# Holding the second group of first loads behind a mask product, and moving one transpose of the next batch behind the first output units, in a fused attention and feed-forward kernel

## The chip, the cores and the metric

The kernel runs on one core of a Trainium2 chip. A core has five engines with a queue of instructions each: TensorE (PE: matrix products and transposes, with its weight loads shown apart as PEld), VectorE (DVE), ScalarE (ACT), GpSimd (POOL) and SyncE (SP). They work at the same time and wait for each other by semaphores. Sixteen DMA engines move data between the large memory (HBM) and the on-chip memory (SBUF); products end in a small memory of their own (PSUM). The metric is the device time of one execution in microseconds (us); lower is better.

## What is computed

Eight batches of eight heads with 576 positions and 64 columns a head go through attention with a sliding window, and the result through a feed-forward layer without gate or bias:

```python
scores = scale * np.matmul(q, k.transpose(0, 1, 3, 2))
mask_plain = (rel >= 0) & (rel < 32)
mask_dil = (rel >= 0) & (rel < 128) & (rel % 4 == 0)
masks = [mask_plain if h < H // 2 else mask_dil for h in range(H)]
attn = softmax(where(masks, scores, -1e9))
x = (attn @ v) with the heads side by side      # 4608 tokens x 512
h = x @ w_in                                    # 512 -> 2048
out = (h * sigmoid(h)) @ w_out                  # 2048 -> 512
```

Half of the heads are "plain": a query sees the 32 positions up to its own. The other half is dilated: a query sees every fourth position, 32 of them. Positions with the same remainder modulo four form a class, and within a class a dilated head is a plain one of 144 positions.

## The kernel before

The order of all work is written out by hand (`tc.manual_schedule()`): each engine runs its instructions in the order in which the Python code issues them. In names of tiles and functions `z` is 0 for the plain heads and 1 for the dilated ones; `b` is the batch.

Attention is done in blocks of 32 queries against 64 keys. For each batch and each kind of head there are these steps: load q and k with a cast to 16 bits, turn them so that the 64 columns lie on partitions (`transpose`: TensorE transposes into PSUM, then a copy per half into `qT`, `kT` or `qC`, `kC`), products of queries and keys (`scores`), mask and row maximum on VectorE, exponentials on ScalarE (`exps`), normalisation and a transpose on VectorE (`normal`, `turned`), products with the values (`values`) and the copy of their result into `xT` (`finish`). The feed-forward layer of a batch has 16 hidden units (`layer1`, for batch 0 `layer1_part`, each 128 of the 2048 columns) with a Silu on ScalarE, and then output units (`layer2`, for batches 0 and 1 together four tiles of 128 tokens in `layer2_first`, 16 units of four products each).

A batch's attention is spread between the feed-forward products of the batch before it. `plan_of(b)` is a table of steps: `at(s, function, ...)` puts a piece of work ahead of unit `s`. Steps 0 to 15 stand ahead of the hidden units, 16 to 31 ahead of the output units; negative steps belong to batch 0 alone.

Batch 0 has nothing to hide behind, so its start is written out at the end of the kernel. Its q and k come in two parts of positions, 0 to 255 and 256 to 575 (`load_part`, into memory that later holds the hidden units, `gT`). The first products of a part add the mask: `mask0` multiplies a unit matrix with the tile `mask_b` into PSUM, and `scores0` adds the scores. The order of the first steps is: mask and scores of the dilated heads, then `mask0(0, 0)` and scores of the plain heads, transposes of k's second part, then of q's second part.

All loads are issued by GpSimd, in this order before the change: k and q of part 0, k of part 1, values of dilated heads 0 and 1, q of part 1, values of dilated heads 2 and 3 (`load_v1`), then values of plain heads 0 and 1 (`load_v0`), the first quarter of `w_in` (`load_w_in`), values of plain heads 2 and 3, two more quarters of `w_in`, and k of batch 1's dilated heads (`load_one`). Eight loads may be under way: a load waits for the landing of the one eight places before it. Everything later (`loads_held`) stands behind a tiny memset into a tile that VectorE and ScalarE use, so that GpSimd waits until that tile is no longer read:

```python
nc.gpsimd.memset(att(0)["l", 0, 1][0:1, 0:1], 0.0)
```

The lines that matter below: L135 `load_part`, L174 `load_v1`, L186 `load_v0`, L199 `load_w_in`, L298 the transposes of batches 1 and on, L302 their copies for plain heads, L335 the copies of batch 0, L392 plain scores, L426 masking, L453 `mask0`, L600 to L630 normalisation and transpose of probabilities, L661 value products, L704 filler products (`warm`), L765 and L786 hidden units of batch 0, L807 output units of batch 0, L859 the memset of `loads_held`.

Of the kernel before, what the change touches and what calls it, by code (L numbers as in the profile page):

```python
# [19 lines left out]
NEG = -1.0e9  # L20
# [9 lines left out]
def kernel(  # L30
# [9 lines left out]
    nc = tc.nc  # L40
    B, H, S, D = q.shape
    DM, DFF = moe_w_in.shape
    scale = 1.0 / (D ** 0.5)
# [32 lines left out]
    mask_b = cpool.tile([P, 2, KB], BF16, name="mask_b")  # L76
# [15 lines left out]
    def tiles_qk(b):  # L92

        for which in (0, 1):
            t = nat.tile([P, GN[0] * QB + GN[1] * GW], F16, tag=f"n{which}", name=f"n{which}_{b}")
            sq = [
                t[:, 0 : GN[0] * QB].rearrange("p (g e) -> p g e", e=QB),
                t[:, GN[0] * QB :].rearrange("p (g e) -> p g e", e=GW),
            ]
            t = t[:, 0 : 2 * sum(URS) * D].rearrange("p (u d) -> p u d", d=D)  # L100
            u0, u1 = 2 * URS[0], 2 * (URS[0] + URS[1])
            qk[b, 0, which] = t[:, 0:u0].rearrange("p (h u) d -> p h u d", h=2)
            qk[b, 1, which] = t[:, u0:u1].rearrange("p (h u) d -> p h u d", h=2)
            for z in (0, 1):
                if b >= DT[z]:
                    qk[b, z, which] = sq[z]

    def load_one(b, z, which):

        src = (q, k)[which]  # L110
        if z == 0:
            nc.gpsimd.dma_start(
                out=qk[b, z, which].rearrange("p h u d -> p h (u d)"),
                in_=src[b, z * HH : z * HH + HH].rearrange("(h i) (p u) d -> (i p) h (u d)", i=2, u=URS[z]),
            )
            return
        for i in (0, 1):
            h = HH + 2 * i
            nc.gpsimd.dma_start(
                out=qk[b, z, which][i * HF : i * HF + UPS[z]].rearrange("p h u d -> p h (u d)"),  # L120
                in_=src[b, h : h + 2].rearrange("h (p u) d -> p h (u d)", u=URS[z]),
            )
# [60 lines left out]
    def load_v0(b, heads=range(HH)):  # L183

        for h in heads:
            nc.gpsimd.dma_start(  # L186
                out=vws[b % 2][h * QB : h * QB + QB, 0:NB], in_=v[b, h].rearrange("(m p) d -> p m d", p=QB)
            )
# [9 lines left out]
    def load_w_in(c):  # L198
        nc.gpsimd.dma_start(  # L199
            out=w_in16[:, :, c * FC : (c + 1) * FC],  # L200
            in_=moe_w_in[:, c * FC : (c + 1) * FC].rearrange("(c p) f -> p c f", p=P),
        )
# [24 lines left out]
    load_v1(0, (0, 1))  # L227
    load_part(0, 1)
    load_v1(0, (2, 3))
    load_v0(0, (0, 1))  # L230
    load_w_in(0)
    load_v0(0, (2, 3))
    for c in (1, 2):
        load_w_in(c)
    tiles_qk(1)
    load_one(1, 1, 1)

    for kt, kc, qc in zip(kTs, kCs, qCs):
        nc.vector.memset(kc[:, :, :, 0:W], 0.0)
# [177 lines left out]
    def width(b, z, g):  # L417

        if b == 0:
            return 8 + g * (4 if z else 2)  # L420
        return 10 if z or g else 8
# [11 lines left out]
    def mask0(z, part, idle=0):  # L433

        n = (2, 3)[part]
        w = width(0, z, part)
        sd = big.tile([P, 16, KB], F32, tag="big", name=f"s0_{z}_{part}")
        bank = sd[:, 0:8].rearrange("p t c -> p (t c)")
        if z:
            sd = sd.rearrange("p (m t) c -> p m t c", m=2)  # L440
            if part:
                parts = [(sd[:, m, 0 : 2 * n], mask_b[:, 1:2].broadcast_to([P, 2 * n, KB])) for m in (0, 1)]
            else:
                pair = mask_b.rearrange("p t c -> p (t c)")[:, None, :].broadcast_to([P, 2, 2 * KB])
                parts = [(sd[:, m, 0:4].rearrange("p (e t) c -> p e (t c)", e=2), pair) for m in (0, 1)]
        elif part:
            parts = [(sd[:, o : o + x], mask_b[:, 1:2].broadcast_to([P, x, KB])) for o, x in ((0, 8), (8, 2))]
        else:
            parts = [(sd[:, 0], mask_b[:, 0]), (sd[:, 1:8], mask_b[:, 1:2].broadcast_to([P, 7, KB]))]
        for i, (t, x) in enumerate(parts):  # L450
            if i == 0:
                warm(bank, idle)
            nc.tensor.matmul(  # L453
                t, ident4.rearrange("p h q -> p (h q)"), x,
                start=bool(z or part or i == 0), stop=True, skip_group_check=not (z or part),
            )
        att(0)["s", z, part] = sd

    def scores0(z, part):

        n = (2, 3)[part]
        w = width(0, z, part)
        sd = att(0)["s", z, part]
        if z:
            for t in range(n):
                for e in (0, 1):
                    for h in range(HH):
                        for m in (0, 1):
                            score_class(0, h, 2 * e + m, 2 * part + t, sd[:, m, e * n + t], False)
        else:  # L470
            for j in range(w):
                for h in (0, 2, 1, 3):
                    score(0, h, 8 * part + j, sd[:, j], False)
        att(0)["raw", z, part] = sd[:, :, 0 : 2 * n] if z else sd[:, 0:w]
# [226 lines left out]
    def warm(t, n):  # L701

        for _ in range(n):
            nc.tensor.matmul(  # L704
                t, ident, ident[:, None, :].broadcast_to([P, 512 // P, P]),
                start=True, stop=True, skip_group_check=True,
            )
# [131 lines left out]
    dve, act = nc.vector.tensor_copy, nc.scalar.copy  # L839
    both = (dve, act)  # L840

    def transposes(at, b, z, step, copies=both):
        for which in (1, 0):
            if b >= DT[z]:
                at(step, turn_qk, b, z, which)
                continue
            at(step, transpose, b, z, which, copies)
# [20 lines left out]
    def plan_of(b):  # L868
        ev = {}

        def at(s, fn, *args):
            ev.setdefault(s, []).append((fn, args))

        def all_exps(b, z):
            for hi in (0, 1):
                at(16, exps, b, z, hi)

        if b == 0:

            at(-8, values0, 1, 1)  # L880
            at(-8, loads_held)
            at(-8, finish0, 1, 1, (act, dve))
            at(-6, values0, 0, 1)
            at(-6, finish0, 0, 1)
            at(0, build_mask)
            at(1, load_qk, 2)
            transposes(at, 1, 1, 6)
            at(10, scores, 1, 1, 0)
            at(11, scores, 1, 1, 1)
            at(13, transpose, 1, 0, 1, both)  # L890
            at(15, transpose, 1, 0, 0, both)
            at(11, shift, 1, 1, 0)
            at(17, scores, 1, 0, 0)
            at(19, scores, 1, 0, 1)
            at(15, load_qk, 3)
            at(15, load_v, 2)
            all_exps(1, 1)
            for hi in (0, 1):
                at(20, exps, 1, 0, hi)
            later(at, 1, 1, (20, 21, 24, 27), (act, act))  # L900
            later(at, 1, 0, (23, 24, 28, 31), (act, dve))
        elif b == 1:
            at(16, load_v, 3)
            transposes(at, 2, 0, 4)
            transposes(at, 2, 1, 6)
            at(10, scores, 2, 0)
            transposes(at, 3, 0, 11, (dve, dve))
            at(17, load_qk, 4)
            at(15, scores, 2, 1)
            all_exps(2, 0)  # L910
            all_exps(2, 1)
            at(17, scores, 3, 0)
            later(at, 2, 0, (21, 24, 27, 28))
            at(22, shift, 3, 0, 0)
            at(22, exps, 3, 0, 0)
            at(22, exps, 3, 0, 1)
            later(at, 2, 1, (29, 30, 33, 34), both)
        else:
            if b + 2 < B:
                at(16, load_v, b + 2)  # L920
            if b + 1 < B:
                later(at, b + 1, 0, (0, 0, 4, 6))
                transposes(at, b + 1, 1, 7)
                if b + 3 < B:
                    at(16, load_qk, b + 3)
            if b + 2 < B:
                transposes(at, b + 2, 0, 14)
                at(19, scores, b + 2, 0)
                at(20, exps, b + 2, 0, 0)
                at(20, exps, b + 2, 0, 1)  # L930
            if b + 1 < B:
                at(12, scores, b + 1, 1)
                if b + 2 == B:
                    at(14, shift, b + 1, 1, 0)
                all_exps(b + 1, 1)
                later(at, b + 1, 1, (22, 23, 27, 28))

        def plan(s):
            for fn, args in ev.pop(s, ()):
                fn(*args)  # L940

        return plan
# [15 lines left out]
    shift0(1, 0)  # L958
    exps(0, 1, 0)
    mask0(0, 0)  # L960
    scores0(0, 0)
    max0(0, 0)
    scaled(0, 0)
# [81 lines left out]
```

## Time and profile before

| | |
|---|---|
| time, median of 3 runs | 303.81 us (303.81 to 304.36) |
| the profiled execution's own time | 304.1 us |
| its span | 302.3 us |
| PE busy | 292.3 us, 97% |
| ACT busy | 203.3 us, 67% |
| DVE busy | 192.7 us, 64% |
| POOL busy | 118.9 us, 39% |
| first product of PE | 5.46 us |
| PE's share of the chain that ended last | 94% |

The span runs from the first to the last instruction; about 1.8 us of the execution lie around it. The first 5.5 us pass before the first load has landed. From then on PE is busy nearly without a break, so a time is gained or lost where PE waits in the first 55 us, and the later part only repeats. The page's forty slices tell nothing that fine; the chain in order of time and the timelines of the single engines do. A load's line shows GpSimd's time to issue it; its landing comes later, and is given as "us to landing". PE's own instructions are brought by a DMA queue too, queue 8 of the page.

### The profile page before, as it was taken

The page shows a single profiled execution, that of the slowest core. Times are in us where ns is not written, and L with a number is a line of the kernel's source. Part 1 is how long each engine was busy: PE and PEld are TensorE (multiplying, and loading weights), DVE is VectorE, ACT ScalarE, POOL GpSimd, SP SyncE. Part 2 cuts the span into 40 slices and gives each one's busy share as a digit, 9 for nine tenths or more (in the row PEclk, how much of TensorE's full clock was granted, in tenths as well). Part 3 has the DMA queues.
Part 4 walks back from the last instruction along what each step waited for, and adds up shares of the span by engine and source line. Part 5 has one row for each costly group of instructions (what it writes and reads, how often), then busy time and mean ns, then how long its engine had stood idle before and what let it go on. Part 6 is the DMA issues. An engine that isn't in the chain of part 4 may idle for free.

```text
span 302.3 us, 10281 instructions
## 1 busy us (share of the span) xinstructions
PE 292.3 (97%) x4395; PEld 186.0 (62%) x4395; DVE 192.7 (64%) x358; ACT 203.3 (67%) x684; POOL 118.9 (39%) x182
## 2 busy tenths in 40 slices
PE   2999999999999999999999999999999999999995
PEld 2667744677446774577545775477644775477543
DVE  1886669559997868776893768856893765800012
ACT  3677689775998659956894559975795568246200
POOL 8709228868898394427705095240000000000000
PEclk9999999999999999999999999999999999999999
DMA  8998999999999899499939199390002000210021
GB/s 103 172 200 124 192 202 137 219 150 138 134 162 184 96 84 147 96 100 51 132 81 160 37 69 132 108 119 2 2 35 106 37 2 23 84 37 0 13 94 69
DMA packets 113213, 30.47 MB, mean 101 GB/s; under 512 B 95520, under 2 KB 108688, under 8 KB 113168
## 3 DMA queue, kind: packets, MB, share of 16 engines
q0 software_dynamic: 107840, 20.38, 85.8%
q1 hardware_dynamic: 5328, 9.44, 8.7%
q8 instruction: 34, 0.56, 0.8%
q14 instruction: 11, 0.09, 0.1%
HBM read 40.75 MB, written 9.44 MB: 166 GB/s over the span
## 4 chain that ended last, share of the span: by engine, by line
PE 94%; DMA 2%; POOL 1%; issue 1%; ACT 0%; DVE 0%; POOLq 0%
PE o L831 37%; PE h L745 37%; PE h L786 5%; PE o L807 5%; PE x L661 4%; DMA gT<-in_q_dram 2%; PE s L382 2%; PE t L298 1%; PE s L392 1%; POOL gT L135 1%; PE h L765 1%; PE s L408 0%; PE ss L382 0%; POOL vw L174 0%; PE h L704 0%
## 5 line engine op out<-in xcount | busy, mean ns | idle before, releaser
L753 ACT ACTIVATE gT<-h 128x576 f16<-128x576 f32 x112 | 72.8, 650 | 63.2 <-PE h L745 63.1
L831 PE MATMUL o<-w_out,gT 128*128 128x512 f16 (+2 forms) x528 | 113.8, 373 | 0.0
L745 PE MATMUL h<-xT,w_in 128*128 128x288 f16 x896 | 113.2, 287 | 0.0
L745 PEld LDWEIGHTS <-w_in 128*128 128x128 f16 x896 | 86.4, 98 | 23.4
L831 PEld LDWEIGHTS <-gT 128*128 128x128 f16 x528 | 50.0, 98 | 56.1
L592 ACT ACTIVATE pe<-ms,nm 128x64 f32<-128x64 f32 x238 | 78.9, 333 | 0.1
L816 DVE COPY ob<-o 128x512 f32<-128x512 f32 (+2 forms) x35 | 23.0, 666 | 51.7 <-PE o L831 50.6
L592 ACT ACTIVATION_READ_ACCUMULATOR pe<-ms,nm 128x1 f32 x238 | 44.6, 187 | 0.0
L152 POOL DMA_DIRECT2D n<-in_k_dram x44 | 32.0, 744 | 26.4 <-DVE kC L355 24.0
L426 DVE SCALAR_TENSOR_TENSOR ms<-s,mask 128x512 f32<-128x512 f32 x28 | 19.2, 686 | 26.6 <-PE s L382 19.5
L152 POOL DMA_DIRECT2D n<-in_q_dram x44 | 32.1, 748 | 3.8 <-DMA n<-in_q_dram 2.2
L174 POOL DMA_DIRECT2D vw<-in_v_dram x32 | 18.3, 580 | 31.4 <-PE x L661 25.0
L614 DVE TENSOR_TENSOR pn<-pe,r 128x640 f16<-128x640 f32 (+2 forms) x32 | 25.3, 792 | 1.1
L630 DVE STREAM_TRANSPOSE pt<-pn 128x640 f16<-128x640 f16 (+4 forms) x32 | 24.7, 772 | 1.1
L186 POOL DMA_DIRECT2D vw<-in_v_dram x32 | 21.2, 674 | 9.0 <-DMA w_out<-in_moe_w_out_dram 8.9
L506 DVE TENSOR_REDUCE nm<-ms 128x10 f32<-128x640 f32 (+1 forms) x28 | 21.9, 786 | 0.9
L661 PEld LDWEIGHTS <-vw 32*64 32x64 f16 (+1 forms) x1264 | 12.9, 107 | 6.7 <-issue 5.4
L786 PE MATMUL h<-xT,w_in 128*128 128x320 f16 (+1 forms) x120 | 16.5, 288 | 0.0
L694 DVE CAST xT<-x 128x288 f16<-128x288 f32 x26 | 10.1, 450 | 8.2 <-PE x L661 8.2
L661 PE MATMUL x<-pt,vw 32*64 32x64 f16 (+2 forms) x1264 | 14.9, 193 | 0.4 <-issue 0.4
L807 PE MATMUL o<-w_out,gT 128*128 128x512 f16 x64 | 14.7, 380 | 0.0
L786 PEld LDWEIGHTS <-w_in 128*128 128x128 f16 x120 | 11.1, 98 | 3.3 <-DMA w_in<-in_moe_w_in_dram 0.2
(102 smaller groups left out, 207.5 us busy)
## 6 DMA issues: line engine op xcount, KB each, us to landing
out_dram<-ob SPq DMA_DIRECT2D x35, 256.0 KB, 3.4
n<-in_k_dram POOLq DMA_DIRECT2D x24, 108.0 KB, 5.0
n<-in_q_dram POOLq DMA_DIRECT2D x24, 108.0 KB, 4.8
vw<-in_v_dram POOLq DMA_DIRECT2D x31, 80.0 KB, 4.1
vw<-in_v_dram POOLq DMA_DIRECT2D x32, 72.0 KB, 4.2
w_in<-in_moe_w_in_dram POOLq DMA_DIRECT2D x4, 512.0 KB, 8.5
w_out<-in_moe_w_out_dram POOLq DMA_DIRECT2D x4, 512.0 KB, 14.9
n<-in_k_dram POOLq DMA_DIRECT2D x20, 72.0 KB, 5.1
```

Source lines behind the costliest of these rows:

```text
L152: nc.gpsimd.dma_start(out=qk[b, z, which][o : o + QB], in_=bass.AP((q, k)[which].tensor, (b * H + z * HH + half * HH // 2) * S * D + x * Q ...
L506: nc.vector.tensor_reduce(out=nm[:, 0:w], in_=ms[:, 0:w], axis=AX.X, op=ALU.max, negate=True)
L592: nc.scalar.activation(pe[:, t, :], src[t], AF.Exp, bias=a["nm", z, hi][:, t : t + 1], scale=k, accum_out=l[:, t : t + 1],)
L614: nc.vector.tensor_tensor(pn[:, 0:w], a["pe", z, hi][:, 0:w], r[:, 0:w, None].broadcast_to([P, w, KB]), ALU.mult)
L630: nc.vector.transpose(out, src)
L661: nc.tensor.matmul(x[h // 2][h % 2 * D : h % 2 * D + D, col : col + wd], vws[b % 2][r, NB + kb * DIL + c if z else kb], turned_cols(b, pt[ ...
L745: nc.tensor.matmul(h[:, half, 0:HS], w_in16[:, c, f * P : f * P + P], xT[c // 2][:, c % 2, half * HS : half * HS + HS], start=(c == cs[0]) ...
L753: nc.scalar.activation(gT[:, f, s0 : s0 + S].rearrange("p (a c) -> p a c", a=2), h[:, :, 0:HS], AF.Silu)
L786: nc.tensor.matmul(hs[i // m][:, i % m, 0 : c1 - c0], w_in16[:, c, (f + i) * P : (f + i + 1) * P], xT[c // 2][:, c % 2, c0:c1], start=(c = ...
L807: nc.tensor.matmul(o, gT[:, f, t * P : (t + 1) * P], w_out16[:, f, :], start=(f == 0), stop=(f == NFF - 1),)
L816: copy(ob, o)
L831: nc.tensor.matmul(o[:, 0, 0:m], gT[:, f, t * P : (t + 1) * P], w_out16[:, f, cols], start=(f == 0), stop=(f == NFF - 1),)
```

## The change

Two edits. First, the loads from the plain values of batch 0 on are put into a function `loads_second`, which is called right after `mask0(0, 0)`. It begins with a memset by GpSimd of one element of `mask_b`, with the value that is there already. That element is read by the mask product, so GpSimd waits for the product before it issues those loads. The order of the loads among each other stays. Second, in batch 0's plan the transpose of batch 1's plain q goes from step 15 (ahead of the last hidden unit) to step 17 (ahead of the second output unit), and both of its copies are made by VectorE (`(dve, dve)`), where one was ScalarE's. The two halves of the plain scores go from steps 17 and 19 to 19 and 20.

```diff
     load_v1(0, (2, 3))
-    load_v0(0, (0, 1))
-    load_w_in(0)
-    load_v0(0, (2, 3))
-    for c in (1, 2):
-        load_w_in(c)
-    tiles_qk(1)
-    load_one(1, 1, 1)
+
+    def loads_second():
+
+        nc.gpsimd.memset(mask_b[0:1, 0, 0:1], NEG / scale)
+        load_v0(0, (0, 1))
+        load_w_in(0)
+        load_v0(0, (2, 3))
+        for c in (1, 2):
+            load_w_in(c)
+        tiles_qk(1)
+        load_one(1, 1, 1)
...
             at(13, transpose, 1, 0, 1, both)
-            at(15, transpose, 1, 0, 0, both)
+            at(17, transpose, 1, 0, 0, (dve, dve))
             at(11, shift, 1, 1, 0)
-            at(17, scores, 1, 0, 0)
-            at(19, scores, 1, 0, 1)
+            at(19, scores, 1, 0, 0)
+            at(20, scores, 1, 0, 1)
...
     mask0(0, 0)
+    loads_second()
     scores0(0, 0)
```

## The prediction

> **What bounds the kernel now.** I read the page first (busy shares, chain), then the chain in order of time, then the first 55 us engine by engine, because the chain holds no wait worth naming behind them.
>
> ```profile
> span 302.3 us, 10281 instructions
> PE 292.3 (97%) x4395; PEld 186.0 (62%) x4395; DVE 192.7 (64%) x358; ACT 203.3 (67%) x684; POOL 118.9 (39%) x182
> PE 94%; DMA 2%; POOL 1%; issue 1%; ACT 0%; DVE 0%; POOLq 0%
> q8 instruction: 34, 0.56, 0.8%
> ```
>
> TensorE (PE) carries 94% of the chain. Whatever the change does must show as PE work starting earlier or later; the last line is the queue that brings PE's own instructions, used below. The chain in order of time has three pieces that are not PE work once the first product has begun:
>
> ```profile
> 5.63 7.20 DMA gT<-in_q_dram
> ...
> 13.62 0.70 ACT qC L335
> ...
> 15.21 0.35 issue
> ...
> 39.07 0.44 issue
> ```
>
> The first is the load of q's second part, which lands at 12.82 and ends a PE gap of 0.54 us. The second and third are gaps in which PE waits for nothing that the page names. The trace's packets of queue 8 name it: each is 16 KB of PE's instructions, 256 of them. One ran from 13.20 to 14.17 and the gap ended at 15.57; another ran from 37.12 to 38.07 and the gap ended at 39.51. Both gaps end 1.4 us after a fetch does, and they fall on the instructions numbered 450 and 1474 of PE's stream, which lie 4 x 256 apart. So PE had run out of instructions. A fetch is asked for when PE crosses the boundary before (9.30 and 33.13 here) and started 3.9 and 4.0 us later, while the load queue was full; at 22.8, where it was nearly drained, the lag was nil. After 39.51 the chain is PE alone but for 0.02 us, so any shift that survives at 55 us is the change in the total.
>
> What POOL issues, and the one weight load of PE that waits for it:
>
> ```profile
> 7.50 1.34 POOL L186 DMA_DIRECT2D vw<-in_v_dram  x2
> 8.82 0.79 POOL L199 DMA_DIRECT2D w_in<-in_moe_w_in_dram  x1
> 9.57 1.35 POOL L186 DMA_DIRECT2D vw<-in_v_dram  x2
> 13.11 1.52 POOL L199 DMA_DIRECT2D w_in<-in_moe_w_in_dram  x2 [2.18 <-DMA gT<-in_q_dram]
> ```
>
> ```profile
> 21.52 1.64 PEld L786 LDWEIGHTS <-w_in 128*128 128x128 f16 x16 [0.20 <-DMA w_in<-in_moe_w_in_dram]
> ```
>
> The three w_in chunks land at 17.44, 21.48 and 23.64 (issue plus 8.6, 8.4 and 9.8 us to landing). PE wants them at 17.48, 21.44 and 24.00. The second one binds already: its first product starts at 21.53, 0.09 us late, and it is the point that decides how much of an early gain lives.
>
> VectorE (DVE) and PE around the moved transposes:
>
> ```profile
> 39.91 0.76 DVE L302 COPY qT<-t 128x576 f16<-128x576 f16 x1 [1.05 <-PE t L298]
> 41.80 0.69 DVE L426 SCALAR_TENSOR_TENSOR ms<-s,mask 128x512 f32<-128x512 f32 x1 [1.14 <-PE s L392]
> 43.98 0.69 DVE L426 SCALAR_TENSOR_TENSOR ms<-s,mask 128x512 f32<-128x512 f32 x1 [0.76 <-PE ss L392]
> 45.64 0.81 DVE L600 TENSOR_REDUCE l<-pe 128x10 f32<-128x640 f32 x1
> 49.84 0.85 DVE L630 STREAM_TRANSPOSE pt<-pn 128x640 f16<-128x640 f16 x1
> ```
>
> ```profile
> 50.91 0.88 PE L661 MATMUL x<-pt,vw 32*64 32x64 f16 x80
> ```
>
> From 45.64 on DVE runs without a pause to the transposed probabilities at 50.69. PE's value products start 0.22 us after that; their first 20 use the half that was ready at 48.63, the rest the one of 50.69. This slack is small.
>
> **Part one, the loads held.** Added: one GpSimd memset (0.09 us, the 1x1 memset of line 859) and its wait for PE's plain mask product, which ends at 9.21 (8.61 + 0.60). From that memset's start to the next issue is 0.24 us in the row of line 859, so the first plain value load is issued at about 9.5 instead of 7.50: 2.0 us late. Behind it in POOL's queue stand four value loads (0.67 us each) and the first w_in chunk (0.79): w_in chunk 0 is issued at 10.85 instead of 8.82, the last value load ends at 13.0. The second chunk waited in any case until 13.11 for the landing at 12.82, so POOL's idle 2.18 us take up the delay, and chunks 1 and 2 and the k loads behind them are issued when they were. No other queue is passed: SyncE issues nothing before 54 us.
>
> What the 2.0 us cost depends on whether the queue runs dry. Lower end, nothing: each DMA engine takes its packets in order, and by the landings engine by engine the quickest one is done with the class values at 11.62, the slowest at 13.47. The first k load had its first packet 1.5 us after its issue (1.25 to 2.77), so the plain values are there at 11.0 and w_in chunk 0 at 12.35, where the quickest engine reached them at 11.62 and 12.59. Upper end, landing moves with issue: chunk 0 at 19.45, 2.0 us late. I take 0, with 0.2 to 0.6 us to spare. Below nothing: the packets of q's second part were slowed (123 GB/s in 9 to 10 against 195 in 7 to 8; engines finish between 10.72 and 12.82). If holding the loads takes that away, chunk 1 lands up to 2.6 us earlier, since the quickest engine had its share of it at 18.88.
>
> Gaps in front: q earlier gains only 0.06 us, since ScalarE is busy with exponentials to 13.56 and starts the copy of the transposed q at 13.62 anyway. The instruction gap of 0.35 may close, as less stands in the queue at 9.30. But PE would then come to chunk 1 at 21.0 and wait for 21.48. So with the landings as they are the front gives 0.0.
>
> **Part two, q's transposes moved.** The 36 transposes now stand behind the last hidden unit (0.65) and the first output unit (0.86). Instruction 1474 then comes at about 40.4, past the 39.5 at which its chunk is there: the gap of 0.44 is gone. One copy moves from ScalarE (0.64) to DVE (0.76). By the chain's pieces: 38.82 + 0.65 + 0.86 + 0.41 (36 k transposes) = 40.74 for the transposes' end; copies on DVE 40.8 to 42.2; two output units (1.83) end at 42.57, so the copies are hidden with 0.35 to spare and would cost PE directly beyond that; scores 42.57 to 42.91, one unit (0.92), scores half two to 44.24. PE is about 0.5 us ahead of before. DVE is not: its first masking moves from 41.80 to 42.99, the maximum runs 43.72 to 44.41, the second masking goes from 43.98 to 44.33. The row from 45.64 follows 0.35 later and the probabilities end at 51.04 in place of 50.69. The first 20 value products go early, the 21st waits until 51.08; before it started at 50.91 + 0.20 = 51.11. So the gap of 0.44 comes back as a wait for DVE: net -0.03, with ends -0.44 (if DVE lost nothing) and +0.15 (transposes taking the 0.60 that they took in two pieces). The value products of the plain heads at 55.34 need DVE's 54.77 + 0.35 = 55.12 only in their second half: no wait. ScalarE gains 1 us that nobody waits for: the probabilities' sums it feeds are read by DVE in order.
>
> Sum: 0.0 - 0.03. The profiled run took 304.1 (span 302.3 and 1.8 around it), 0.3 above the median of 303.81; on the median the forecast is 303.8, its own range 303.5 to 304.2.
>
> **Rivals.**
> (a) The slow stretch of the queue eases and chunk 1 lands early. For it: POOL issued values and w_in all through that stretch. Against: it issued as steadily from 4 to 8 at 183 to 198 GB/s. Gain: 0.09 + 0.35 + 0.06 = 0.5 from the waits. More if the products of 17.45 to 20.73 go at full pace: eight of 256 columns took 1.77 us there, 0.22 each, and 24 of them 2.71 us right after, 0.113 each; with the two fillers 1.4 us less. ScalarE caps it near 1.0: its Silu that ends at 25.66 is needed by PE around 26.3 (0.65 to spare), and its own chain comes only the 0.35 earlier. So -0.3 to -1.0, middle 303.2.
> The Trainium skill (DMA: Bandwidth & Descriptors, Latency and other measured facts) puts slow DMA engines down, as a best guess, to GpSimd's descriptor rings sharing their ports; by that rule case (a) would be the likely one, while the 183 to 198 GB/s under the same issuing do not agree.
> (b) The other side: the queue runs dry between 11.6 and 12.6 and w_in chunk 0 lands late. It decides from about 17.6 on, as PE's weight load stands at 17.48 with 0.2 to spare. For it: after an empty queue, packets took 300 ns instead of 135 at 24.0. Price 0.5 to 2.0, middle 304.9.
> (c) PE's slow pace lasts longer. The page's granted clock reads full in every slice, so the pace is read from the durations just given: slow to about 20.4, full after. As long a stretch again (17.45 to 20.73, 3.3 us) at half pace does half its work: +1.65, 305.5. Only that step speaks for it.
> The Trainium skill (TensorE: Matmul & The Clock Gate, Part 1) says that PE runs at half clock until a free-running window of 3.4 us was busy; that agrees with 0.22 and 0.113, and lets the step fall a window earlier (case a) or later (case c).
> (d) The move does not do what it is for: the two copies end behind 42.57 or the instruction gap stays, +0.3 to 0.5, 304.2.
>
> **Numbers.** Forecast 0.46, (a) 0.32, (b) 0.12, (c) 0.05, (d) 0.05. The bound of 0.2% is 0.6 us (303.2 and 304.4), about what a measurement of this kernel can tell from no change. Faster: 0.22 of (a) and 0.01 of the forecast; slower: (b), (c), 0.02 of (d), 0.01 of the forecast; the rest is the same. Range 303.0 to 304.9: it leaves out 0.08 of (a), half of (b) and (c), 0.19 in all.
>
> **What would show it.** In the profile after: POOL's memset near 9.3 and value loads from 9.5; w_in chunk 1 issued near 13.1; the weight load at 21.5 still waiting for it; no "issue" gap at 39; a PE wait for DVE of about 0.5 us inside the value products near 51. If the wait at 21.5 is gone, (a) holds; a wait for w_in near 17.5 is (b).

## The result and the profile after

The changed kernel takes 304.56 us in the median of 22 executions, the kernel before 303.81 us in the median of 22. The ratio is 1.0032 with a 95% interval of 1.0021 to 1.0044: slower by 0.75 us, where 303.8 and no measurable change had been forecast. A second set later gave 1.0039 (1.0018 to 1.0061).

The profiled execution took 304.15 us with a span of 302.2 us, a little quicker than its median. Its page:

```profile
span 302.2 us, 10284 instructions
PE 291.6 (96%) x4395; PEld 185.7 (61%) x4395; DVE 193.1 (64%) x359; ACT 202.7 (67%) x683; POOL 119.0 (39%) x183
PE 89%; DMA 5%; DVE 3%; POOL 1%; issue 0%; POOLq 0%
```

TensorE (PE) is busy 291.6 us instead of 292.3, and its share of the chain that ended last falls from 94% to 89%. The chain now runs through loads for 5% (2% before) and through VectorE for 3% (0% before); PE's own waits, shown below, are shorter than these shares. The two issue gaps of before are gone. What GpSimd (POOL) issues, as the timeline of that engine shows it (start, duration, line, operation, idle time before it and what ended that):

```profile
8.97 0.09 POOL L233 MEMSET mask_b<- 1x1 bf16 x1 [1.42 <-PE s L457]
9.21 1.34 POOL L186 DMA_DIRECT2D vw<-in_v_dram  x2
10.53 0.78 POOL L199 DMA_DIRECT2D w_in<-in_moe_w_in_dram  x1
12.61 1.53 POOL L199 DMA_DIRECT2D w_in<-in_moe_w_in_dram  x2
```

The loads are issued 1.7 us later (2.0 had been worked out), and w_in's chunk 1 no later than before (12.61 against 13.11), since POOL's idle time has absorbed the delay, as forecast. PE's waits, in its timeline (the lines stand four further down than before, so L790 is the L786 of the kernel before):

```profile
14.51 0.62 PE L412 MATMUL s<-kC,qC 64*32 64x64 f16 x48 [0.79 <-ACT qC L339]
21.15 1.92 PE L790 MATMUL h<-xT,w_in 128*128 128x256 f16 x16 [0.51 <-DMA w_in<-in_moe_w_in_dram]
24.05 1.05 PE L790 MATMUL h<-xT,w_in 128*128 128x256 f16 x8 [0.37 <-DMA w_in<-in_moe_w_in_dram]
50.33 0.34 PE L665 MATMUL x<-pt,vw 32*64 32x64 f16 x20
51.02 0.71 PE L665 MATMUL x<-pt,vw 32*64 32x64 f16 x60 [0.36 <-DVE r L615]
```

PE waits 0.51 us for chunk 1, which binds as before, and 0.37 us for chunk 2, which had not bound. In the value products it waits 0.36 us for VectorE. VectorE's chain behind that last wait:

```profile
40.74 1.42 DVE L306 COPY qT<-t 128x576 f16<-128x576 f16 x2 [1.82 <-PE t L302]
42.95 0.69 DVE L430 SCALAR_TENSOR_TENSOR ms<-s,mask 128x512 f32<-128x512 f32 x1 [0.79 <-PE s L396]
45.93 0.81 DVE L604 TENSOR_REDUCE l<-pe 128x10 f32<-128x640 f32 x1
50.12 0.84 DVE L634 STREAM_TRANSPOSE pt<-pn 128x640 f16<-128x640 f16 x1
```

The chain from the sums at 45.93 on is 0.29 us later than the 45.64 before; a shift of 0.35 had been worked out. By this one execution nearly everything went as written: PE starts the first layer-one product of batch 1 at 56.87 us, against 56.92 before. Yet the median is 0.75 us up. So a single trace of each kernel could not answer the question, and further traces of both were taken with the experiments.

### The profile page after: what moved, and what is told of

It reads as the page before. It is cut to its first block, busy times and chain, and to the rows that moved or that the text cites. A ratio compares the mean times of both kernels' runs of the same rounds, so it can differ in the third digit from the quotient of the medians.

```text
span 302.2 us, 10284 instructions
## 1 busy us (share of the span) xinstructions
PE 291.6 (96%) x4395; PEld 185.7 (61%) x4395; DVE 193.1 (64%) x359; ACT 202.7 (67%) x683; POOL 119.0 (39%) x183
## 4 chain that ended last, share of the span: by engine, by line
PE 89%; DMA 5%; DVE 3%; POOL 1%; issue 0%; POOLq 0%
PE o L835 37%; PE h L749 37%; PE h L790 4%; PE x L665 4%; DMA w_in<-in_moe_w_in_dram 4%; PE o L811 2%; PE s L386 2%; DMA gT<-in_k_dram 1%; POOL vw L186 1%; PE t L302 1%; DVE pt L634 1%; DVE pn L618 1%; DVE ms L430 0%; DVE nm L510 0%; POOL w_in L199 0%
## 5 line engine op out<-in xcount | busy, mean ns | idle before, releaser
L430 DVE SCALAR_TENSOR_TENSOR ms<-s,mask 128x512 f32<-128x512 f32 x28 | 19.2, 686 | 25.5 <-PE s L386 19.5
L790 PE MATMUL h<-xT,w_in 128*128 128x320 f16 (+1 forms) x120 | 16.4, 287 | 0.9 <-DMA w_in<-in_moe_w_in_dram 0.9
L790 PEld LDWEIGHTS <-w_in 128*128 128x128 f16 x120 | 11.1, 98 | 4.5 <-DMA w_in<-in_moe_w_in_dram 1.2
```

What stands on the lines that cost most here:

```text
L790: nc.tensor.matmul(hs[i // m][:, i % m, 0 : c1 - c0], w_in16[:, c, (f + i) * P : (f + i + 1) * P], xT[c // 2][:, c % 2, c0:c1], start=(c = ...
```

## The experiments

Three theories were on the table at first: H (the held loads make w_in late), D (the moved transposes lose to VectorE's chain) and C (PE's slow pace at the start lasts longer). F (PE starves for instructions) was added later. S and P, at the end, split H further.

Two marks make the traces comparable: the start of w_in's product number 40 (counted from 0), with which all three chunks have been in use, and the stretch from there to the first layer-one product of batch 1, which holds part two. From that product to the end each of the sixteen traces takes 245.4 us, so what is gained or lost shows in one of the two. Landings are the last of a load's sixteen completion marks, one of each DMA engine; the "middle engine" is their median.

### The two parts alone, and both kernels again

The first is the kernel before, the second the changed kernel, unedited. The third has part one alone:

```diff
-    load_v0(0, (0, 1))
-    load_w_in(0)
...
+    def loads_second():
+        nc.gpsimd.memset(mask_b[0:1, 0, 0:1], NEG / scale)
+        load_v0(0, (0, 1))
+        load_w_in(0)
...
     mask0(0, 0)
+    loads_second()
```

The fourth has part two alone:

```diff
-            at(15, transpose, 1, 0, 0, both)
+            at(17, transpose, 1, 0, 0, (dve, dve))
-            at(17, scores, 1, 0, 0)
-            at(19, scores, 1, 0, 1)
+            at(19, scores, 1, 0, 0)
+            at(20, scores, 1, 0, 1)
```

> The kernel before, run once more for its spread and a second trace. All theories: a median near 303.8 us. Theory C (the changed kernel's executions differ in how long TensorE keeps its slow pace) expects that nearly all executions of this kernel show one and the same mean granted clock, and that their times lie within 1 us; theory H (the held loads land late) and theory D (the moved transposes make TensorE wait for VectorE) say nothing of the clock.

> The changed kernel once more, for its spread and a second trace. All theories: a median near 304.6 us, with a second group of executions near 305.4. Theory C: the second group has a lower mean granted clock (0.988 to 0.994) than the first (0.999 to 1.0). Theories H and D: the groups don't differ in the clock, and the time is lost in a wait for a w_in chunk near 17 to 24 us (H) or near 51 us (D).

> The held loads alone; the transposes and copies of batch 1's plain q stay at step 15 as before. Theory H: the whole loss is here, +0.7 us or more against the kernel before. Theory D: 0.0, no loss. Theory C (the filled gaps in front shift where the activity of TensorE is judged busy): +0.7 or more too, with the same two groups in time and clock as the changed kernel.

> The moved transposes and VectorE's copies alone; the loads are issued as before. Theory D: the whole loss is here, +0.7 us. Theories H and C: within 0.2 us of the kernel before, as in the forecast (-0.03 us: the instruction gap at 39 us gone, a wait for VectorE at 51 us in its place).

| kernel | median us (12 executions) | ratio to before, 95% interval |
|---|---|---|
| before | 303.54 | 0.9991 (0.9978 to 1.0004) |
| changed | 304.78 | 1.0039 (1.0018 to 1.0061) |
| part one alone | 304.32 | 1.0013 (0.9999 to 1.0028) |
| part two alone | 303.98 | 1.0006 (0.9990 to 1.0021) |

The larger share is part one's, but neither interval leaves out 1.0. D had put the whole loss, 0.7 us, into part two; that is 1.0023 and just outside part two's interval. C had expected a lower mean granted clock in the changed kernel's slower executions; of the twelve here five took 305 us or more, and four of these had 0.998 to 1.0. It had also expected the kernel before to stay within 1 us, and that spread over 1.5 us with clocks of 0.998 to 1.0. Part one alone, from PE's timeline:

```profile
21.99 1.92 PE L790 MATMUL h<-xT,w_in 128*128 128x256 f16 x16 [0.65 <-DMA w_in<-in_moe_w_in_dram]
39.82 0.35 PE L302 MATMUL t<-ident,n 64*64 64x64 f16 x20 [0.22 <-issue]
```

And part two alone:

```profile
50.65 0.71 PE L661 MATMUL x<-pt,vw 32*64 32x64 f16 x60 [0.36 <-DVE r L611]
```

Each part brings its own wait, and only that one. The second trace of the kernel before has no issue gap at 39 at all; part one alone has 0.22 us there. The 0.44 us that part two was to remove thus differ from execution to execution.

The second trace of the changed kernel (304.82 us) shows something else. Its stretches, by engine, with the granted clock, the DMA share (packets under way per DMA engine, on average) and GB/s as the last three columns:

```profile
12.20:15.61 3.41, 2.02 (x107) 1.60 (x106) 2.98 (x8) 3.41 (x16) 3.04 (x5) 1.00 1.26 159
15.61:22.44 6.83, 6.38 (x94) 3.85 (x93) 5.98 (x12) 5.09 (x25) 0.01 (x1) 0.50 1.37 189
```

PE was granted the full clock for one stretch of 3.41 us, in which it was busy for only 2.02 us, and then half of it for two. PE waited 0.45 us for chunk 0; chunk 1's arrival at 21.26 cost nothing there, the slow pace did. That is C, as a fall back to the half clock, in one execution.

### Released early, released late

To separate the delay from the added instruction, the same memset and wait were kept and only their place was changed: first behind batch 1's plain mask product, which PE ends near 7.2 us, then behind the transposes that it ends near 10.5 us.

```diff
     mask0(1, 0)
+    loads_second()
...
     mask0(0, 0)
-    loads_second()
```

> Part one alone as in the run of part one by itself, but the same loads behind the same added memset are released by the batch's other plain mask product (batch 1's), which PE ends near 7.2 us: the values are issued at about 7.5, as before. It keeps the added wait and takes the delay away. H (the delay itself makes w_in's chunks late): w_in's chunks 1 and 2 land near 21.1 and 23.4 again (21.13 and 23.40 on average in the three traces without the delay, 21.44 and 24.15 in the three with it), q's second part near 12.8 again, no wait of PE for chunk 2, about 303.7 us. The rival (what costs is the added instruction and its wait in GpSimd's queue, or code that has moved): stays near the 304.3 of part one alone. C (PE's slow pace): no statement; it goes with where gaps of PE fall.

```diff
-        nc.gpsimd.memset(mask_b[0:1, 0, 0:1], NEG / scale)
+        nc.gpsimd.memset(ident[0:1, 1:2], 0.0)
...
     mask0(0, 0)
-    loads_second()
...
     transpose0(1, 1, 1, dve)
+    loads_second()
```

> Part one alone with a longer delay: the loads are released by the transposes of k's second half in batch 0, which PE ends near 10.5 us, so the values are issued at about 10.8, 1.6 us later than in the change and 3.3 later than before. Held behind a memset of one element of the identity (zero onto zero) on GpSimd. H (the delay makes w_in's chunks late): the loss grows; chunk 0 of w_in, issued near 12.2 in place of 10.5, lands 0.5 to 1.6 later than 17.6, PE waits for it where it had not, and the run takes 304.9 to 306. The rival that a queue this long hides any delay of its entries: w_in lands as in the change, 304.3.

Early: 303.70 us, ratio 0.9999 (0.9984 to 1.0013). Late: 305.18 us, 1.0048 (1.0029 to 1.0067). So the added memset and its wait cost nothing that these runs show; the delay does, and more delay costs more. The time of the early release is the one that H gave, its trace is not: chunks 1 and 2 landed at 19.94 and 22.50, about 1 us earlier than H had said, and q's second part at 11.42 instead of 12.8. POOL with the early release:

```profile
7.50 0.09 POOL L233 MEMSET mask_b<- 1x1 bf16 x1
7.54 1.37 POOL L186 DMA_DIRECT2D vw<-in_v_dram  x2
9.20 0.77 POOL L199 DMA_DIRECT2D w_in<-in_moe_w_in_dram  x1 [0.28 <-DMA gT<-in_k_dram]
```

POOL and PE with the late one:

```profile
10.85 0.09 POOL L233 MEMSET ident<- 1x1 f16 x1 [3.31 <-PE t L321]
12.41 0.79 POOL L199 DMA_DIRECT2D w_in<-in_moe_w_in_dram  x1
19.18 0.61 PE L769 MATMUL h<-xT,w_in 128*128 128x256 f16 x4 [2.06 <-ACT pe L596]
```

With the late release chunk 0 lands at 19.14 and PE starts on it at 19.18, after 2.06 us of idleness. The profile names ScalarE as releaser; the landing 0.04 us before the start says that it was the load. The edit also made PE itself wait for this memset, 0.21 us near 11, because the transposes behind it read `ident`; that is hidden in the 2.06 us.

### Two more traces of the changed kernel

> The changed kernel once more, for a third trace of it. H: w_in's chunks 1 and 2 land near 21.4 and 24.1 (21.13 and 23.40 without the delay), PE waits for one or both by 0.3 to 0.7 us; wait for VectorE of 0.36 us near 51. If the time is 305 or above, either a stretch of half clock between 15 and 23 (C) or an instruction gap of about 1 us near 26 (F; as in the trace with the fillers, 1.14 us at 26.00) is in the trace, and the other is not.

> The changed kernel once more, for a fourth trace of it: as for the third.

They took 305.34 and 304.66 us, with no instruction gap between 16 and 44 us and no fall back of the clock. Both take the form of H, with different chunks late and waits longer than the 0.3 to 0.7 us expected. The third trace of the changed kernel, PE's timeline:

```profile
18.86 1.03 PE L769 MATMUL h<-xT,w_in 128*128 128x256 f16 x4 [1.13 <-DMA w_in<-in_moe_w_in_dram]
```

The fourth:

```profile
21.95 1.92 PE L790 MATMUL h<-xT,w_in 128*128 128x256 f16 x16 [1.24 <-DMA w_in<-in_moe_w_in_dram]
```

In the third, chunk 0 was there only at 18.81, against 17.44 in the first profile of before; fifteen of its engines had finished by 17.24, one came 1.6 us later. In the fourth, chunk 1 came at 21.90. The expectation had allowed a time above 305 only by C or F; here it came mainly from the late chunk. PE starts on chunk 0 1.08 us later than in the first profile of before and on product 40 1.23 us later (26.66 against 25.43). The slow pace has a part all the same: the full clock was granted only at 21.78 us here, against 18.17 in the fourth trace, which shows in the same four products of the third and the fourth trace,

```profile
20.79 1.03 PE L769 MATMUL h<-xT,w_in 128*128 128x256 f16 x4
19.06 0.61 PE L769 MATMUL h<-xT,w_in 128*128 128x256 f16 x4
```

so the third one could not make up for its wait. The mean granted clock of 1.0 in both does not tell that apart: it counts all time ahead of the first recorded step as full.

### Fillers against the slow pace

Two filler products were put into the changed kernel where PE waits 0.79 us for the copy of q near 14.

```diff
     transpose0(0, 0, 1, act)
+    att(0)["bank", 0, 1] = big.tile([P, 16, KB], F32, tag="big", name="s0_0_1")
+    warm(att(0)["bank", 0, 1][:, 0:8].rearrange("p t c -> p (t c)"), 2)
     scores0(1, 1)
```

> The changed kernel with two filler products of 512 columns more, put where PE waits some 0.8 us for the copy of the transposed q near 14 us. They compute nothing that is used. C (a second group of executions at 305 and above comes from PE's pace stepping up a window early and falling back for two windows because of that idle time): no execution with a mean clock below 0.998, where 11 or 12 of 34 of the changed kernel had one below 0.996; the median falls by 0.2 to 0.3, to about 304.3, the upper group is gone. H: the waits for w_in's chunks near 21.2 and 24.0 stay, and with them 304.5 against 303.8. If the fillers push PE's work (they outlast the wait): up to 0.3 later at 15, hidden again by the waits for w_in.

304.97 us, 1.0043 (1.0027 to 1.0059). None of 10 executions had a mean clock under 0.998, and still 5 of them took 305 or more. In the trace the full clock was granted from 12.14 on without a fall back: PE was busy for 2.48 of the first 3.41 us, where the trace that fell back had 2.02. C is not needed for the loss. It was a poor test in one way: the fillers themselves waited until 13.98 for their PSUM tile, so they filled less than meant. The wait for w_in stayed, in PE's timeline:

```profile
21.27 1.92 PE L792 MATMUL h<-xT,w_in 128*128 128x256 f16 x16 [0.58 <-DMA w_in<-in_moe_w_in_dram]
```

and the chain of waits shows a new gap:

```profile
26.00 1.14 issue
```

A chunk of PE's instructions had come from 24.70 to 25.60, and the gap ended at 27.14, 1.5 us after it: the same signature as the two gaps of before. That is F. It is nearly the whole loss of this trace: with the faster pace product 40 starts at 25.17, no later than in the two traces of before (25.43 and 25.24), in spite of the wait for w_in. In the early-release trace it appears at 32.23 (PE's timeline):

```profile
32.79 0.22 PE L412 MATMUL s<-kC,qC 64*32 64x64 f16 x8 [0.56 <-issue]
```

That execution had been 0.90 us ahead of the second trace of before at product 40 (24.34 against 25.24) and was even with it at batch 1's layer one (56.12 against 56.10). The gap took 0.56 of it.

### The moved transposes in two other forms

The first keeps the place of the transposes but gives the copies back to both engines and draws the scores nearer:

```diff
-            at(15, transpose, 1, 0, 0, both)
+            at(17, transpose, 1, 0, 0, both)
-            at(17, scores, 1, 0, 0)
+            at(18, scores, 1, 0, 0)
```

> Part two in another form, without part one: batch 1's plain q is transposed behind layer two's first units as in the change, but its two copies go to VectorE and ScalarE as before, and the two halves of the scores follow at the next two places instead of two and three places later. D (the moved transposes lose to VectorE's chain what they win at the instruction gap): VectorE's chain from the masking on is not later than before, so no wait of 0.36 us for it inside the value products near 51, and no instruction gap near 39; from w_in's product number 40 to the first layer-one product of batch 1 PE takes 30.9 to 31.0 us, against 31.38 in the three traces with the move as changed and 31.49, 30.86 and 31.27 in the three without; about 303.4 to 303.6 us. If the two transposed blocks' copies on two engines now hold PE up instead (the case that the move doesn't do its job): 31.4 again and 303.9.

309.49 us, 1.0199 (1.0177 to 1.0221): far outside both expectations. The cause is the edit itself, and it tells why the change uses VectorE for both copies. ScalarE, with the exponentials of step 16 ahead in its queue:

```profile
41.59 0.74 ACT L581 ACTIVATE pe<-ms 128x640 f32<-128x640 f32 x1
45.54 0.61 ACT L302 COPY qT<-t 128x576 f16<-128x576 f16 x1
```

PE, behind that copy:

```profile
46.21 0.61 PE L392 MATMUL s<-kT,qT 64*32 64x64 f16 x30 [4.30 <-ACT qT L302]
```

From step 17 on, a copy on ScalarE stands behind 4 us of exponentials, and PE waits for it; around that wait it was also granted half the clock, from 44.72 to 51.55 us. The second form therefore puts the transposes at step 16, ahead of those exponentials, and leaves the scores alone:

```diff
-            at(15, transpose, 1, 0, 0, both)
+            at(16, transpose, 1, 0, 0, both)
```

> Part two in a third form, without part one: batch 1's plain q is transposed one unit later than before (behind the last hidden unit, ahead of the first output unit), its copies on VectorE and ScalarE and ahead of the exponentials in ScalarE's queue, the scores where they were. D (in the change the moved transposes lose to VectorE's chain what they win at the instruction gap): PE comes to instruction 1474 about 0.65 us later, near 39.3 to 39.7, when its chunk is there, so no instruction gap near 39; VectorE's masking is not later than before, so no wait of 0.36 us for it inside the value products near 51; from w_in's product number 40 to the first layer-one product of batch 1 some 30.9 us, in each execution, against 31.38 with the move as changed; 303.3 to 303.6. If the instruction gap only moves to another place: 31.2 to 31.5 and the time of before.

303.54 us, 1.0002 (0.9986 to 1.0017). Its PE timeline:

```profile
39.28 0.56 PE L298 MATMUL t<-ident,n 64*64 64x64 f16 x36
50.34 0.88 PE L661 MATMUL x<-pt,vw 32*64 32x64 f16 x80
```

There is no gap at 39 and no wait in the value products, and the stretch from product 40 on takes 30.94 us, as D expected. The gain of 0.4 us in the trace does not show as a faster median: the same gap is missing in some executions of before too (its second trace takes 30.86). Then the early release and this form were combined:

> The loads behind the added memset but released early (w_in's product number 40 at 24.34 in that trace, 0.9 earlier than in the second trace of before) together with the transposes one unit later. F (PE's instruction chunks cap what an early front is worth: that trace lost 0.56 us at 32.23 to a gap that ended 1.6 us after a chunk had come, and had its layer one of batch 1 at 56.12, no earlier than before's 56.10): the same here, an instruction gap of 0.3 to 0.8 us between 32 and 40, first layer-one product of batch 1 near 56, 303.2 to 303.7. If the front's gain lives: 55.3 and 302.6 to 302.9.

303.39 us, 0.9993 (0.9979 to 1.0006), the lowest median, but not shown to beat the kernel before. The question was not put: in its trace the front was not early (product 40 at 25.22), because PE waited for chunks 1 and 2:

```profile
20.91 1.92 PE L790 MATMUL h<-xT,w_in 128*128 128x256 f16 x16 [0.50 <-DMA w_in<-in_moe_w_in_dram]
23.78 1.05 PE L790 MATMUL h<-xT,w_in 128*128 128x256 f16 x8 [0.34 <-DMA w_in<-in_moe_w_in_dram]
```

That F caps every early front is therefore open; it was seen in one trace. A gap of 0.32 us at 33.00 also stands in the trace with chunk 0 first, below, whose front was not early.

### Why a held load makes later loads late

Chunk 1 is issued no later in the changed kernel, yet lands later on average (the table below; in the first pair of profiles it landed at 21.10 against 21.48). The stretches of the queue, with the same last three columns: the second trace of before,

```profile
11.00:13.00 2.00, 1.25 (x6) 0.29 (x4) 1.90 (x5) 1.93 (x13) 0.00 (x0) 1.00 1.74 142
13.00:15.00 2.00, 1.89 (x72) 1.58 (x72) 1.82 (x6) 1.80 (x7) 1.77 (x3) 1.00 1.21 189
15.00:17.00 2.00, 1.77 (x72) 1.08 (x62) 1.97 (x3) 1.27 (x4) 0.87 (x2) 1.00 1.73 182
```

part one alone,

```profile
11.00:13.00 2.00, 1.96 (x17) 0.88 (x17) 1.90 (x6) 1.77 (x13) 1.96 (x4) 1.00 1.67 138
13.00:15.00 2.00, 1.30 (x72) 1.07 (x76) 1.63 (x6) 2.00 (x9) 2.00 (x4) 1.00 1.25 184
15.00:17.00 2.00, 2.00 (x75) 1.26 (x75) 1.97 (x3) 1.12 (x3) 0.13 (x1) 1.00 1.67 156
```

and the late release:

```profile
11.00:13.00 2.00, 2.00 (x24) 1.30 (x24) 1.90 (x6) 1.86 (x13) 1.92 (x3) 1.00 1.15 117
13.00:15.00 2.00, 1.87 (x86) 1.52 (x87) 1.86 (x6) 2.00 (x8) 2.00 (x4) 1.00 0.97 59
```

With the late release the queue plainly runs short: 59 GB/s. With part one alone it is less obvious: 156 against 182 GB/s from 15 to 17, with nearly as many packets under way (1.67 against 1.73 for each DMA engine). To tell a shortage of bytes (S) from the pattern of POOL's issuing (P), chunk 0 of w_in was taken out of the hold and put ahead of it:

```diff
+    load_w_in(0)
+
     def loads_second():
         nc.gpsimd.memset(mask_b[0:1, 0, 0:1], NEG / scale)
         load_v0(0, (0, 1))
-        load_w_in(0)
         load_v0(0, (2, 3))
```

> Part one alone, but w_in's chunk 0 is issued before the memset, near 7.5, and only the four value loads, chunks 1 and 2 and the k loads stand behind the wait. So 512 KB more lie in the queue while the rest is held. S (the hold costs because the queue runs short of bytes between 9 and 17): from 7 to 17 us the queue moves 1.75 MB or more (1.76 on average in the seven traces without the hold, 1.69 in the six with it), the middle one of the sixteen engines has its share of chunk 1 at 19.4 or before (19.37 without, 19.83 with), chunk 1 is there by 21.1, product number 40 at 25.2, about 303.7. P (the hold costs by where GpSimd issues, in one piece from 9.2 to 16 where before it paused from 10.9 to 13.1, or by what other engines move in that time): the rate of 13 to 17 stays near 168 GB/s (188 without), chunk 1's middle engine 19.8, 304.2 to 304.4.

> Part one alone once more, beside the former on the same chip, for the comparison and a second trace: 304.3 us, chunk 1's middle engine near 19.8 and its last near 21.7, 1.69 MB from 7 to 17 us. If part one were neutral: 303.8.

On the same chip, chunk 0 first took 303.74 us, 1.0003 (0.9989 to 1.0016), and part one alone again 304.06 us, 1.0024 (1.0005 to 1.0044). POOL with chunk 0 first:

```profile
7.52 0.78 POOL L199 DMA_DIRECT2D w_in<-in_moe_w_in_dram  x1
9.24 2.64 POOL L186 DMA_DIRECT2D vw<-in_v_dram  x4
12.95 1.51 POOL L199 DMA_DIRECT2D w_in<-in_moe_w_in_dram  x2 [1.08 <-DMA gT<-in_q_dram]
```

The values are held as in the change and the loss is no longer seen. The times alone do not separate the two kernels, since their intervals overlap from 1.0005 to 1.0016. All traces together (means; GB/s are those of the stretches, MB their sum from 7 to 17 us):

| traces | MB, 7 to 17 us | middle engine's mark for chunk 1 | chunks 0, 1, 2 landed | product 40 |
|---|---|---|---|---|
| seven with loads from 7.5 us (before twice, part two alone, both forms of the move, early release, early release with the move) | 1.76 | 19.37 (18.95 to 19.79) | 17.23, 21.04, 23.46 | 25.19 |
| chunk 0 ahead of the hold | 1.76 | 19.38 | 16.58, 21.16, 23.63 | 25.11 |
| seven held as in the change (changed four times, with fillers, part one alone twice) | 1.68 | 19.88 (19.61 to 20.16) | 17.62, 21.66, 24.24 | 25.85 |
| late release | 1.41 | 21.76 | 19.14, 22.76, 25.47 | 27.29 |

The numbers that S named for this kernel came out within 0.1: 1.76 MB, 19.38, 21.16 and 25.11, in one trace. For product 40 the groups overlap, 24.34 to 25.60 against 25.17 to 26.66. Two things do not fit S alone. From 13 to 17 the rate with chunk 0 first was 176 GB/s, between the 188 of the unheld traces and the 167 of the held ones, and POOL still paused for 1.08 us, so some part for P is not excluded. And from 11 to 17 the held traces move 162 GB/s against 181 on average, 11% less, with only 4% fewer packets under way (1.54 against 1.61 for each DMA engine): most of the shortfall is packets that move fewer bytes in their time, not a queue that stands empty as with the late release.

## Why the prediction was wrong

**The step that failed is part one's price, "I take 0, with 0.2 to 0.6 us to spare".** It asked when the quickest DMA engine would run out of work, from the first packet after an issue. Nothing in the trace had shown how a gap in that supply acts on loads issued later. What the runs show in its place is a price of about 0.5 us for part one alone (304.32 against 303.81 and 304.06 against 303.56, on two chips), paid where PE waits for w_in. Measured over seven traces each, the held kernels move 0.08 MB less by 17 us, at some 190 GB/s about 0.4 us of work; chunk 1 is 0.5 us later on the middle engine, and the chunks land 0.4, 0.6 and 0.8 us later. PE, which had 0.09 us of wait and 0.36 us of slack on chunks 1 and 2 in the profile of before, passes 0.66 us of it on at product 40 (25.85 less 25.19; 0.51 without the early-release trace, which was 0.9 ahead). That is most of the 0.75 us of the medians. The first profile after shows only 0.06 of it (25.49 against 25.43), so the single pair of profiles would have confirmed the 0.

**"Chunks 1 and 2 ... are issued when they were" was right and misleading.** They are even issued 0.5 us earlier in the profile after. But a chunk waits behind the bytes ahead of it: in the first profile of before chunk 1 took 8.4 us from issue to landing, 0.8 us of that POOL's own instruction. The issue time of chunk 1 did not tell its landing here; the bytes that the queue had moved by 17 us went with it.

**Rival (b) was the nearest.** It had w_in late because the queue has too little in it; its "about 17.6" for chunk 0 is the edge on which the changed kernel now sits (17.59, 17.58, 18.81 and 17.72 in its four traces), and the middle of its price, given as 304.9 (0.5 to 2.0 on 303.8 has its middle at 305.05), is close to the 304.56 and 304.78 measured. It was given 0.12. Where it erred is in the point of decision: the loss comes mostly through chunks 1 and 2, and chunk 0 decided only one trace of the four.

**Rival (a)'s premise held and was worth nothing.** With the loads held, q's second part lands 0.4 us earlier (12.05 against 12.48 on average) and the stretch from 9 to 11 us moves more (174 GB/s against 155, seven traces each). PE then waits 0.79 us for ScalarE's copy, as the forecast's "q earlier gains only 0.06" had it. The 0.04 MB that the queue gained from 9 to 11 it lost three times over between 11 and 17.

**Rival (c) is real and not the cause.** The full clock that lasts past product 40 is granted no later with the loads held: between 12.14 and 22.44 us in the seven held traces, 19.0 on average, and between 17.29 and 20.83 in the six of the unheld ones that record a step, 19.5 on average. One of the four traces of the changed kernel falls back to half the clock. Among the 22 executions of the result, ten had a mean granted clock under 0.998, which marks such a fall back, among them all seven between 305.1 and 305.9; the other twelve have a median of 304.46, still 0.65 above before. So the fall back adds some 0.1 us to the median. It also occurs without any hold: the trace with the transposes at step 16 was granted full clock from 12.34, half from 15.75, and full again from 19.17, and took 303.52 us. The Trainium skill (TensorE: Matmul & The Clock Gate, Part 1) puts the clock's decision in free-running windows of about 3.4 us; the stretches here, 3.41 and 6.83 us, agree, and the fall back after a window in which PE was busy for 2.02 of 3.41 us is a case that the forecast did not have; its rival (c) held only a later first step.

**Part two came out as forecast, near zero.** Its "net -0.03" weighed a gap of 0.44 us removed against a wait added. The wait of 0.36 us was there in each of the six traces with the move as changed. In five of them the stretch from product 40 takes the same 31.38 us; with the fillers it took 32.70, the gap of 1.14 in it. The seven traces with the transposes at their old place take 30.86 to 31.81, 31.44 on average. The gap was the term that was taken from one execution: it was 0.44, none, 0.22 and 0.29 in the four of them that have the order of before or part one alone. Rival (d) did not occur in the change. The medians say the same: part two alone 1.0006 (0.9990 to 1.0021).

**What stays open.** The ratios of the two parts alone (1.0013 and 1.0024 for part one, 1.0006 for part two) add up to less than the 1.0032 and 1.0039 of both; the intervals are too wide to tell whether the parts add. Why the held queue moves fewer bytes although nearly as many packets are under way is open. Which of the sixteen engines comes last, and why it trails the middle one by 0.6 to 2.7 us in every load of w_in, was not settled. No kernel run here is shown to be faster than the one before.

The numbers: the time of 304.56 lies in the range that was given, 303.0 to 304.9, but the forecast was 303.8 with 0.57 on no change, and the change came out slower, which had 0.20.

## What to carry to other kernels

Think of a DMA queue that the first weights wait for as a store of bytes: in this kernel, holding an early load to let another one through made later loads late, even those whose issue time did not move. If loads must be held, try putting the largest one that the next stage needs ahead of the hold; here that was enough for the loss not to be seen. And where a change is worth less than a us, read two or three traces of the kernel before, for a gap that one trace shows may not be in the next.

## What was not expected of the hardware

- PE's instructions come in chunks of 256 by a DMA queue, queue 8 of the page. With loads in the queue a chunk started up to 5.3 us after PE had crossed into the chunk before, and each gap that was left ended 1.3 to 1.6 us after its chunk had come. The prediction's rule that PE's crossing asks for the next chunk does not always hold: in the second trace of before one started at 45.98, 1.4 us ahead of the crossing at 47.40. The gaps ranged from 0.2 to 1.14 us and moved from execution to execution (15.21, 26.00, 32.23, 33.00, 39.07, 39.60 us).
- A load of w_in is not done evenly: in the third trace of the changed kernel fifteen engines had their share of chunk 0 between 15.44 and 17.24 us and the last at 18.81. The Trainium skill (DMA: Bandwidth & Descriptors, Why a DMA increments its semaphore by 16 and not by 1) says that the engines of a load finish independently and that only the full count means that the data is there; the sixteen marks agree, and it was this last engine, not the quickest on which the forecast's margin was built, that PE waited for.
